# Filler matmuls at the start of TensorE's queue, and two small loads moved to GpSimd's queue, in an RWKV-and-MLP kernel

## The chip, the cores and the metric

The kernel runs on one core of one Trainium2 chip. The metric is the device time of one execution in microseconds (us). Engines are named as the profile names them: PE is TensorE (matmuls), PEld its weight loads, DVE is VectorE, ACT is ScalarE, POOL is GpSimd, SP is SyncE, which here only issues transfers.

## The reference, cut to what matters

```python
# r, k, v: (4, 8, 768, 48); w, u: (8, 48)
for t in range(S):
    cur = einsum('bhd,bhe->bhde', u[None] * k_t, v_t)
    y[:, :, t] = einsum('bhd,bhde->bhe', r_t, state + cur)
    state = w[None, :, :, None] * state + einsum('bhd,bhe->bhde', k_t, v_t)
x = y.transpose(0, 2, 1, 3).reshape(3072, 384)
out = square(maximum(x @ moe_w_in, 0)) @ moe_w_out     # (384, 2048), (2048, 384)
```

A linear recurrence with a decay w and a bonus u, and then a two-layer block with a squared ReLU.

## The kernel before, in words

The sequence of 768 steps is cut into 6 chunks of 128 for each of 4 batches: 24 units, numbered 4 x chunk + batch. Within a chunk the recurrence is written as masked products, and between the chunks of a batch a state is carried.

Each unit goes through these steps. SP loads r, k and v (L288). DVE multiplies r and k by powers of w (`scale`, L311, once for r and once for k); these powers, `wpos` and `wneg`, come once from a chain at the start: a row of w is loaded by ACT's queue (L205), ACT takes its logarithm (L222), PE spreads it over the partitions in one f32 product (`spread_log`, L260), and ACT raises it (L263). The scaled r and k are transposed, by PE (`turn`, L331, eight 128x128 transposes in two groups of four, each evicted by ACT, L335) for the first seven units, and by a DMA transpose (L320) for the rest. DVE multiplies the transposed pair (`rk`, L340). PE makes the 128x128 products of r and k (`at`, L348), DVE masks them (`mask`, L360, twice). PE makes `sums` (L368 with the columns of u, and L373, which gives what is added to the state). DVE forms `dv` (L382) and the state (`state_add`, L390 in the first chunk, L392 later; `state_decay`, L396), ACT casts the state (L402). PE makes y (L411 and L417), DVE evicts it (L426). y is transposed by PE (L442) with an eviction by ACT (L446), or by a DMA transpose (L435). PE then multiplies by `w_in` (`mm1`, L458, steps of 12 matmuls of 128 columns, or 6 of 256 where two units are taken together), ACT applies the ReLU (L466), DVE or ACT squares (L475, L473), PE multiplies by `w_out` (`mm2`, L482, steps of 4 matmuls of 384 columns; L497 for the last unit), ACT evicts (L489), and SP stores (L519).

Once, near the start, w and u are also loaded as columns: `columns` (L255, L256) issues two loads of 4 x 2 x 48 numbers on SP's queue, `spread_columns` (L268) transposes them on PE in f32, DVE copies them (`copy_columns`, L271), and POOL makes of them the matrix `uwb` for `sums` (L274, L277) and the decay over a chunk, `wend` (L280, L282), for `state_add`.

The weights are loaded in quarters on POOL's queue (`weights`), w_in at L298 and w_out at L302, with a cast to bf16. Before each, POOL copies one number of a unit's k tile (`gate`, L294), so that the weights start after that unit's loads.

The order of all work is not left to a scheduler. Every step is entered in a `Plan` with an engine, a cost, what it needs, a rank and its buffers. `Plan.run` goes through time with these costs and, for each engine, starts the ready step of the lowest rank; the instructions are then emitted in that order, which is the order in which each engine runs them. A step marked `move` is a transfer, with an issue cost and a time to land. The eight PSUM banks are handed out by the plan too, with a limit for each kind. In the order that comes out for PE, log is first, then the first four transposes of unit 0, the column transposes, the other four, and so on; on SP the column loads stand between the loads of unit 0 and unit 1.

Of the kernel before, what the change touches and what calls it, by code (L numbers as in the profile page):

```python
# [149 lines left out]
def kernel(  # L150
# [11 lines left out]
    nc = tc.nc  # L162
# [42 lines left out]
    nc.scalar.dma_start(out=wrow, in_=w.rearrange("h d -> (h d)").unsqueeze(0))  # L205
    nc.scalar.preload_act_table_set("natural_log_exp_and_others")
    wu = const.tile([HP, 2, 2, 64], F32)
    nc.vector.memset(wu[:, 0], 1.0)
# [38 lines left out]

    w_in_sb = const.tile([128, NK, dff], BF16)
    w_out_sb = const.tile([128, NF, dm], BF16)
    gate = const.tile([128, 1], F32)  # L250
# [3 lines left out]
    def columns():  # L254
        nc.sync.dma_start(out=wu[:, 0, :, :D], in_=w.rearrange("(p o) d -> p o d", o=2))  # L255
        nc.sync.dma_start(out=wu[:, 1, :, :D], in_=u.rearrange("(p o) d -> p o d", o=2))  # L256

# [35 lines left out]
    def weights(i, q, which):  # L293
        nc.gpsimd.tensor_copy(gate, tiles[i]["kt"][:, 0, :1])  # L294
        if which == "I":
            sl = slice(q * dff // NQ, (q + 1) * dff // NQ)
            src = moe_w_in.rearrange("(ko ki) f -> ki ko f", ki=128)
            nc.gpsimd.dma_start(out=w_in_sb[:, :, sl], in_=src[:, :, sl])  # L298
        else:
            sl = slice(q * NF // NQ, (q + 1) * NF // NQ)  # L300
            src = moe_w_out.rearrange("(ko ki) f -> ki ko f", ki=128)
            nc.gpsimd.dma_start(out=w_out_sb[:, sl, :], in_=src[:, sl, :])  # L302

# [144 lines left out]
    def mm1(i, m, s):  # L448
        c, b = units[i]
        t = tiles[i]  # L450
        if b == 0 and s == 0:
            chunks[c]["g"] = gpool.tile([128, NF, B, C], BF16, name="g")
        t["h", s] = bank("h", i, s).rearrange("p (a u c) -> p a u c", u=m, c=C)
        for a in range(4 // m):
            f = s * (4 // m) + a
            for n in range(NK):
                turned = w_in_sb[:, n, f * 128 : (f + 1) * 128]
                nc.tensor.matmul(  # L458
                    out=t["h", s][:, a], lhsT=turned, rhs=chunks[c]["xT"][:, n, b : b + m, :],
                    start=(n == 0), stop=(n == NK - 1),  # L460
                )
# [15 lines left out]
    def mm2(i, q):  # L477
        t = tiles[i]
        if q == 0:
            t["o"] = bank("o", i)[:, :dm]  # L480
        for f in range(q * 4, q * 4 + 4):
            nc.tensor.matmul(  # L482
                out=t["o"], lhsT=chunks[units[i][0]]["g"][:, f, units[i][1], :], rhs=w_out_sb[:, f, :],
                start=(f == 0), stop=(f == NF - 1),
            )
# [5 lines left out]
    def mm2_half(i, n):  # L491
        t = tiles[i]
        if n == 0:
            t["o"] = bank("o", i)[:, :dm]
        sl = slice(n * dm // 2, (n + 1) * dm // 2)
        for f in range(NF):
            nc.tensor.matmul(  # L497
                out=t["o"][:, sl], lhsT=chunks[units[i][0]]["g"][:, f, units[i][1], :], rhs=w_out_sb[:, f, sl],
                start=(f == 0), stop=(f == NF - 1), skip_group_check=True,
            )  # L500
# [34 lines left out]
    copy("begin", SP, 0.74, None, rank=-1e3)  # L535
    copy("wu", SP, 1.46, columns, rank=-99.75, move=(0.1, 16, 0.67, 0.1))
    add("cols", PE, 0.1, spread_columns, rank=-50, needs=["wu"], new=[("h", "cols")])
# [141 lines left out]
    )  # L679
    for s in plan.run(room, dict(at=4, s=2, y=2, h=4, o=2), len(banks)):  # L680
        if s["emit"] is not None:
# [31 lines left out]
```

## Time and profile before

| what | us |
|---|---|
| three runs | 180.97, 183.15, 185.44 |
| their median | 183.15 |
| the profiled execution | 179.87 |
| its span, first to last instruction | 178.1 |
| PE busy | 163.5 |
| DVE busy | 144.8 |
| ACT busy | 118.8 |
| POOL busy | 12.4 |

The profile is one execution. A line of instructions in order of time gives the start, the busy time, the engine, the source line, the operation, what it writes and reads with shapes, how many instructions were merged, and in brackets how long the engine had stood idle before and what released it. An engine name with a q (SPq, POOLq) is its queue of transfers. DVE, ACT and POOL run their instructions in the order given; a wait at the head of a queue holds up all that stands behind it.

### The profile page before, as it was taken

Reading aid. Unit: us, or ns where it says so; the run is one execution under the profiler, and the core shown is the slowest. Engines: PE = TensorE matmul, PEld = TensorE weight load, DVE = VectorE, ACT = ScalarE, POOL = GpSimd, SP = SyncE. Lnnn points to the kernel's source line nnn. Section 1 sums busy time; section 2 is a strip of 40 time slices with the busy share of each in tenths; the row PEclk is TensorE's granted clock in tenths of the full one; section 3 lists DMA queues with packets and bytes.
Section 4 is the critical chain, followed back from the end, with each engine's and each line's share of the span. In section 5 each row is a group of like instructions: output and inputs, shape, how many; then the busy total and the mean of one; then the engine's idle time right before and its main releaser. Section 6 shows DMA issues by size and latency. Waiting matters only on the chain.

```text
span 178.1 us, 4914 instructions
## 1 busy us (share of the span) xinstructions
PE 163.5 (92%) x1982; PEld 125.2 (70%) x1982; DVE 144.8 (81%) x307; ACT 118.8 (67%) x240; POOL 12.4 (7%) x38
## 2 busy tenths in 40 slices
PE   2477889999999999999999999998999999999992
PEld 1356679886687886686786775784875788777771
DVE  4398998855899999999799999998998799762310
ACT  4546889987464965696694594694691897746620
POOL 3250950000000000000000000000000000000000
PEclk9999999999999999999999999999999999999999
DMA  5899999999955889999998899999999999811212
GB/s 116 161 184 202 171 200 187 184 202 184 129 107 95 155 158 197 118 207 213 137 206 180 167 193 159 207 188 135 222 199 137 216 163 208 235 47 26 90 62 70
DMA packets 107680, 28.56 MB, mean 160 GB/s; under 512 B 100873, under 2 KB 107658, under 8 KB 107658
## 3 DMA queue, kind: packets, MB, share of 16 engines
q1 hardware_dynamic: 103944, 25.11, 79.7%
q0 software_dynamic: 3712, 3.15, 11.0%
q8 instruction: 15, 0.25, 0.6%
q14 instruction: 7, 0.06, 0.1%
q10 hardware_dynamic: 2, 0.00, 0.0%
HBM read 20.45 MB, written 4.72 MB: 141 GB/s over the span
## 4 chain that ended last, share of the span: by engine, by line
PE 59%; DMA 21%; DVE 11%; ACT 3%; issue 2%; SPq 2%; ACTq 0%
PE bank L458 26%; PE bank L482 20%; DMA rkT<-rkw 12%; DMA xT<-yb 4%; PE bank L348 3%; DMA rt<-in_r_dram 3%; DVE rkw L311 3%; DMA kt<-in_k_dram 2%; PE bank L331 2%; DVE am L360 2%; DVE g L475 2%; PE bank L411 2%; DVE yb L426 2%; PE bank L497 1%; ACT rkT L335 1%
## 5 line engine op out<-in xcount | busy, mean ns | idle before, releaser
L458 PE MATMUL bank<-xT,w_in_sb 128*128 128x128 bf16 (+1 forms) x864 | 73.4, 238 | 0.3
L482 PE MATMUL bank<-w_out_sb,g 128*128 128x384 bf16 x368 | 68.3, 326 | 0.0
L466 ACT ACTIVATE gr<-bank 128x512 f32<-128x512 f32 x96 | 55.0, 594 | 18.9 <-PE bank L458 16.3
L458 PEld LDWEIGHTS <-w_in_sb 128*128 128x128 bf16 x864 | 61.2, 98 | 7.5 <-issue 0.5
L475 DVE TENSOR_TENSOR g<-gr 128x512 bf16<-128x512 f32 x64 | 43.1, 685 | 12.9 <-ACT gr L466 12.8
L482 PEld LDWEIGHTS <-g 128*128 128x128 bf16 x368 | 33.3, 98 | 18.1 <-DVE g L475 0.2
L360 DVE TENSOR_TENSOR am<-bank,smask 128x512 bf16<-128x512 f32 x48 | 31.7, 684 | 1.1 <-PE bank L348 0.7
L402 ACT CAST stb<-st 64x192 bf16<-64x192 f32 x40 | 13.9, 348 | 15.5 <-DVE st L396 14.6
L473 ACT ACTIVATE g<-gr 128x512 bf16<-128x512 f32 x32 | 20.1, 632 | 0.8
L489 ACT COPY osb<-bank 128x384 f32<-128x384 f32 x23 | 11.0, 478 | 8.4 <-PE bank L482 8.1
L311 DVE TENSOR_TENSOR rkw<-rt,wpos 128x384 bf16<-128x384 f32 x24 | 13.2, 550 | 3.0 <-ACT wpos L263 2.5
L426 DVE TENSOR_TENSOR yb<-bank,dv 128x384 bf16<-128x384 f32 x24 | 13.3, 553 | 1.3 <-PE bank L417 0.9
L311 DVE TENSOR_TENSOR rkw<-kt,wneg 128x384 bf16<-128x384 f32 x24 | 13.2, 551 | 1.3 <-DMA kt<-in_k_dram 1.3
L382 DVE TENSOR_TENSOR dv<-vb,bank 128x384 f32<-128x384 bf16 x24 | 13.1, 546 | 0.5 <-PE bank L373 0.5
L348 PE MATMUL bank<-rkT 64*128 64x128 bf16 x192 | 10.2, 229 | 3.6 <-ACT rkT L335 2.0
L340 DVE TENSOR_TENSOR rk<-rkT 128x512 bf16<-128x512 bf16 x24 | 10.1, 420 | 3.8 <-ACT rkT L335 1.9
L348 PEld LDWEIGHTS <-rkT 64*128 64x128 bf16 x192 | 5.8, 98 | 9.5 <-DMA rkT<-rkw 3.9
L315 ACT CAST vb<-vt 128x384 bf16<-128x384 f32 x24 | 12.2, 509 | 0.2
L335 ACT COPY rkT<-bank 128x512 bf16<-128x512 bf16 x14 | 8.2, 584 | 5.9 <-PE bank L331 5.6
L392 DVE TENSOR_TENSOR st<-bank,st 64x192 f32<-64x192 f32 x32 | 11.3, 352 | 0.2
L331 PE MATMUL bank<-identb,rkw 128*128 128x128 bf16 x56 | 6.7, 256 | 3.6 <-DVE rkw L311 1.8
L411 PEld LDWEIGHTS <-am 128*128 128x128 bf16 x192 | 8.4, 98 | 1.7 <-DVE am L360 0.3
(52 smaller groups left out, 90.2 us busy)
## 6 DMA issues: line engine op xcount, KB each, us to landing
rt<-in_r_dram SPq DMA_DIRECT2D x24, 192.0 KB, 3.1
kt<-in_k_dram SPq DMA_DIRECT2D x24, 192.0 KB, 3.8
vt<-in_v_dram SPq DMA_DIRECT2D x24, 192.0 KB, 4.0
out_dram<-osb SPq DMA_DIRECT2D x23, 192.0 KB, 2.9
w_in_sb<-in_moe_w_in_dram POOLq DMA_DIRECT2D x4, 384.0 KB, 7.6
w_out_sb<-in_moe_w_out_dram POOLq DMA_DIRECT2D x4, 384.0 KB, 13.8
xT<-yb SPq DMA_TRANSPOSE x18, 3.6
rkT<-rkw SPq DMA_TRANSPOSE x17, 3.7
```

Of the source, the lines that this page charges most:

```text
L311: nc.vector.tensor_tensor(t["rkw"][:, x, :, :, :D], pair(src), pair(wx), ALU.mult)
L315: nc.scalar.copy(tiles[i]["vb"], tiles[i]["vt"])
L348: nc.tensor.matmul(out=t["at"][o][:, p, :], lhsT=t["rkT"][sl, 1, p, :], rhs=t["rkT"][sl, 0, p, :], start=True, stop=True,)
L360: nc.vector.tensor_tensor(am, t["at"][o], smask.unsqueeze(1).to_broadcast([C, HP, C]), ALU.mult)
L382: nc.vector.tensor_tensor(t["dv"], t["vb"], t["d"].unsqueeze(2).to_broadcast([C, H, D]), ALU.mult)
L402: nc.scalar.copy(stb[b][sl, :, o * D : (o + 1) * D], st32[b][sl])
L426: nc.vector.tensor_tensor(t["yb"], t["y"], t["dv"].rearrange("p h d -> p (h d)"), ALU.add)
L458: nc.tensor.matmul(out=t["h", s][:, a], lhsT=turned, rhs=chunks[c]["xT"][:, n, b : b + m, :], start=(n == 0), stop=(n == NK - 1),)
L466: nc.scalar.activation(t["gr", s], t["h", s], AF.Relu)
L473: nc.scalar.activation(g, x, AF.Square)
L475: nc.vector.tensor_tensor(g, x, x, ALU.mult)
L482: nc.tensor.matmul(out=t["o"], lhsT=chunks[units[i][0]]["g"][:, f, units[i][1], :], rhs=w_out_sb[:, f, :], start=(f == 0), stop=(f == NF - 1),
```

## The change

A tile `warm` of ones (128 x 256, bf16) is set by DVE first of all. Sixty fillers, each one matmul of 256 columns of that tile by itself into a bank of its own that nothing reads, are entered in the plan for PE with the highest ranks, each needing the one before it, so that they are placed wherever the plan has nothing else ready for PE; the ninth also needs log. The loads of w and u as columns are issued on POOL's queue with a planned issue cost of 4.4 us instead of SP's with 1.46. The weights become one tile for each quarter, with the same transfers and the same reads.

In the order that comes out, PE runs 8 fillers, log, 5 fillers, the column transposes, 2 fillers, the first four transposes of unit 0, 2 fillers, the other four, 5 fillers, the first four transposes of unit 1, 2 fillers, `at` of unit 0, 1 filler, `sums` of unit 0, 1 filler, the other four transposes of unit 1, 8 fillers, `at` of unit 1, y of unit 0, 10 fillers, the x transposes of unit 0, 3 fillers, and so on; all sixty stand ahead of the first step of `mm1`. On DVE the copy of the columns moves ahead of the k scaling of unit 0, the r scaling of unit 1 ahead of `rk` of unit 0. On PE, y of unit 3 moves behind the second-quarter steps of `mm1` of units 0 and 1. On POOL the two column loads follow the memset of `uwb` and stand ahead of the work on the columns and of all weight gates. On SP the loads of unit 1 follow those of unit 0 directly. Later steps keep their kind of order but change places by a step or two on all engines.

```diff
+    warm = const.tile([128, 256], BF16)
+    nc.vector.memset(warm, 1.0)
     wu = const.tile([HP, 2, 2, 64], F32)
...
-    w_in_sb = const.tile([128, NK, dff], BF16)
-    w_out_sb = const.tile([128, NF, dm], BF16)
+    w_in_q = [const.tile([128, NK, dff // NQ], BF16, name=f"w_in_q{q}") for q in range(NQ)]
+    w_out_q = [const.tile([128, NF // NQ, dm], BF16, name=f"w_out_q{q}") for q in range(NQ)]
...
     def columns():
-        nc.sync.dma_start(out=wu[:, 0, :, :D], in_=w.rearrange("(p o) d -> p o d", o=2))
-        nc.sync.dma_start(out=wu[:, 1, :, :D], in_=u.rearrange("(p o) d -> p o d", o=2))
+        nc.gpsimd.dma_start(out=wu[:, 0, :, :D], in_=w.rearrange("(p o) d -> p o d", o=2))
+        nc.gpsimd.dma_start(out=wu[:, 1, :, :D], in_=u.rearrange("(p o) d -> p o d", o=2))
+
+    def fill():
+        nc.tensor.matmul(out=bank("fill")[:, :256], lhsT=warm[:, :128], rhs=warm, start=True, stop=True)
...
-            nc.gpsimd.dma_start(out=w_in_sb[:, :, sl], in_=src[:, :, sl])
+            nc.gpsimd.dma_start(out=w_in_q[q], in_=src[:, :, q * dff // NQ : (q + 1) * dff // NQ])
...
-    copy("wu", SP, 1.46, columns, rank=-99.75, move=(0.1, 16, 0.67, 0.1))
+    copy("wu", POOL, 4.4, columns, rank=-99.75, move=(0.1, 16, 0.67, 0.1))
+    add("made", PE, 1.25, None, rank=-2e3)
+    for n in range(60):
+        add(
+            ("fill", n), PE, 0.215 if n < 16 else 0.108, fill, rank=1e3 + n, needs=[("fill", n - 1) if n else "made", "log" if n == 8 else None],
+            new=() if n else [("fill",)], uses=[("fill",)] if n else (),
+        )
...
-    for s in plan.run(room, dict(at=4, s=2, y=2, h=4, o=2), len(banks)):
+    for s in plan.run(room, dict(at=4, s=2, y=2, h=4, o=2, fill=1), len(banks)):
```

## The prediction, made before the changed kernel was run

> **What bounds the kernel now.** I read the page's slices first, then a table of busy time by stage, then the instructions in order of time through the first 25 us, where all edits lie.
>
> From the page, the span in 40 slices of 4.45 us:
>
> ```profile
> PE   2477889999999999999999999998999999999992
> DVE  4398998855899999999799999998998799762310
> PEclk9999999999999999999999999999999999999999
> ```
>
> The table by stage (stretch, its length, then busy us and instructions of PE, PEld, DVE, ACT, POOL, then clock and DMA):
>
> ```profile
> core 0: us, PE busy (x) PEld busy (x) DVE busy (x) ACT busy (x) POOL busy (x), PEclk, DMA share, GB/s
> 5.40:9.38 3.98, 2.29 (x25) 1.65 (x26) 2.01 (x6) 2.05 (x4) 1.72 (x7) 1.00 1.05 184
> 9.38:15.30 5.92, 4.04 (x47) 3.08 (x45) 5.85 (x13) 3.29 (x8) 1.95 (x6) 1.00 1.27 182
> 15.30:25.00 9.70, 7.84 (x120) 6.40 (x118) 9.12 (x20) 7.90 (x17) 7.24 (x14) 1.00 1.20 193
> 25.00:60.00 35.00, 34.98 (x519) 28.71 (x517) 29.04 (x59) 26.62 (x55) 0.00 (x0) 1.00 0.99 161
> 60.00:160.00 100.00, 98.08 (x1134) 73.60 (x1132) 92.88 (x190) 69.29 (x143) 0.00 (x0) 1.00 0.98 176
> ```
>
> From 25.0 us on TensorE is the bound: 34.98 of 35 us busy, then 98.08 of 100. What the front can give is therefore the moment at which TensorE becomes saturated, about 25 us, and nothing of TensorE's busy time before it counts by itself. From 9.38 to 25 us VectorE is the bound (5.85 of 5.92, 9.12 of 9.70). Before 9.38 it is one chain through all engines.
>
> The instructions in order of time, first 12 us (start, duration, engine, line, idle before and its releaser):
>
> ```profile
> 3.91 0.63 SPq L256 DMA_DIRECT2D wu<-in_u_dram  x1
> 4.59 0.44 SPq L288 DMA_DIRECT2D rt<-in_r_dram  x1
> ...
> 6.04 0.61 PE L331 MATMUL bank<-identb,rkw 128*128 128x128 bf16 x4 [1.27 <-DVE rkw L311]
> ...
> 6.58 0.37 PE L268 MATMUL bank<-ident,wu 4*128 4x4 f32 x2
> ...
> 8.56 0.43 DVE L340 TENSOR_TENSOR rk<-rkT 128x512 bf16<-128x512 bf16 x1 [1.41 <-ACT rkT L335]
> ...
> 10.65 0.92 POOL L298 DMA_DIRECT2D w_in_sb<-in_moe_w_in_dram  x1
> ```
>
> and from 12 to 24 us:
>
> ```profile
> 15.75 0.55 DVE L382 TENSOR_TENSOR dv<-vb,bank 128x384 f32<-128x384 bf16 x1 [0.46 <-PE bank L373]
> ...
> 16.95 1.46 PE L458 MATMUL bank<-xT,w_in_sb 128*128 128x128 bf16 x12
> ...
> 19.00 0.40 PE L331 MATMUL bank<-identb,rkw 128*128 128x128 bf16 x4
> ...
> 19.46 0.83 PE L458 MATMUL bank<-xT,w_in_sb 128*128 128x128 bf16 x12
> ```
>
> and TensorE alone after 24 us:
>
> ```profile
> 24.84 0.27 PE L411 MATMUL bank<-vb,am 128*128 128x48 bf16 x4 [0.24 <-DVE am L360]
> 24.96 2.17 PE L458 MATMUL bank<-xT,w_in_sb 128*128 128x128 bf16 x36
> ```
>
> Here one sees TensorE change speed at about 19 us although the clock row shows 9 throughout: four transposes take 0.61 us before and 0.40 after, twelve L458 matmuls 1.46 and 0.83. The state followed a stretch in which PE was busy 3.20 of 3.41 us (15.69 to 19.10); the two stretches of that length before it, busy 2.38 and 2.51, did not bring it. VectorE stood 1.41 us before rk (L340) and 0.46 us before dv (L382), both behind slow TensorE groups. TensorE's saturated stretch starts at 24.96, right after y of unit 3 had waited 0.24 us for a mask.
>
> **The change part by part.** Times are those of the profiled execution: 179.87 us, span 178.1 and 1.77 around it. It lies under all three runs (180.97, 183.15, 185.44).
>
> 1. *Columns on GpSimd's queue.* GpSimd is free at 2.30 (the uwb memset, 2.17 + 0.13). Its weight loads cost 0.74 to 0.92 us to issue; two of them end at about 4.0. After the issue at 10.65 that queue moved no data until 13.2, that is 2.55 us after the issue began. So the second, issued at about 3.2, moves data at 5.8 and is seen at about 6.2. Lower end: nothing shows a load of 8 rows on this queue; if its issue cost little and it landed as SP's do (3.0 us from issue, median), 5.3. Upper end: as the fastest whole weight load (6.3 us after its issue), 9.5. I take 6.2, since the 1.5 KB behave like the first data of a load, not like all of one. Behind that wait: on TensorE the two column transposes now stand ahead of the first real work (eight fillers, log, five fillers, columns, two fillers, then the first transposes of unit 0); on VectorE the copy of the columns stands ahead of the k scaling of unit 0. Columns 6.2 + 0.37, gap 0.06, two fillers at 0.11 to 0.21 each: the transposes of unit 0 begin at about 6.9 instead of 6.04, **0.9 us late**. On GpSimd itself nothing is delayed: it waited 4.94 us for the copied columns before (7.24), and what is queued behind (uwb, wend, the first weight gate) follows the copy, now at about 6.7 instead of 6.99; the first weight load goes out at about 10.3 instead of 10.65.
> 2. *On SP* the two issues go (1.18 + 0.63, from 2.68 to 4.59). Unit 1's r is issued at about 2.7, and later loads move up by some 0.8 us, since the DMA engines were busy except about 4.8 to 5.8. That covers the loads which the first weight gates read (the second gate waited 5.75 us for k of unit 3, to 17.31). w_in's second quarter comes about 0.7 us earlier. Worth nothing alone: hidden by VectorE's stage, but it keeps the weights from being late when the rest moves up.
> 3. *TensorE faster early.* Eight fillers from about 1.1 to 2.9, log 3.13 to 4.77, five fillers to 5.8: TensorE is nearly always busy, so the full speed should come before 9 us rather than at 19. A transpose group then costs 0.40 instead of 0.61, the eight L348 matmuls 0.40 (21.65) instead of 0.61. Two transpose groups stand in the chain before rk: 2 x 0.21 = 0.4 back of the 0.9. rk starts at about 8.56 + 0.5 = 9.05.
> 4. *VectorE's new order.* The r scaling of unit 1 (pitch 0.47) moves ahead of rk, into the idle 1.41 us. So dv of unit 0 starts 2.0 us after rk, not 2.48: 11.05, against 11.04 before. Parts 1, 3 and 4 cancel: **0.0** (ends: -0.8 if the columns land at 5.3, +3.3 if at 9.5).
> 5. *VectorE's gaps.* From 9.38 to 25 it stood 0.07 + 0.58 = 0.65 us, of which 0.46 before dv of unit 1 behind slow groups. At full speed most of it closes: **-0.5** (ends: 0 and -0.65).
> 6. *Order before saturation.* y of unit 3 and its 0.24 us wait move behind two w_in steps; the steps of units 0 and 1 on the second quarter start after the transposes of unit 4. The 0.24 wait and part of the 0.27 behind it come off: **-0.4** (ends 0 and -0.5). The remaining TensorE work is the same.
> 7. *Sixty fillers.* All stand before the first w_in step. Between 9.38 and 15.3 TensorE was idle 5.92 - 4.04 = 1.88 us. At full speed the 4.04 shrinks by about a third, to some 2.7, leaving 3.2; the 30 or so fillers there cost 30 x 0.107 = 3.2 (a slow step of 12 x 128 columns took 1.46, with some 0.2 for the last one to come out: 0.105 for 128 columns, 0.21 for a filler's 256, half of it at full speed). They just fit: **+0.1** (ends 0 and +1.7, one stretch of 3.4 us at half speed).
> 8. *Tiles for each quarter of the weights*: the same transfers and reads of the same shapes. The first w_in step ran at 16.95 before the second quarter was issued (17.77), so no wait hangs on the single tile: 0.
> 9. *The memset of warm* (0.17, as L208) lies in VectorE's idle 2.55 us before 5.42: 0.
>
> Sum: 0.0 - 0.5 - 0.4 + 0.1 = -0.8; w_in's earlier quarter allows it. The planner lists later steps in a changed order too: work ahead of each unit's steps on TensorE shifts by up to one w_in step, 0.65 us, either way. 179.87 becomes about 179.1. The four executions shown average (179.87 + 180.97 + 183.15 + 185.44)/4 = 182.36; less 0.8 and a little for runs in which TensorE sped up later than in this profile, I forecast 181.4 for the median of runs.
>
> [...]
>
> [...]
>
> **The rivals.**
>
> *A. The columns land late (slower).* Place: head of TensorE's queue. Every microsecond past 6.2 delays unit 0, and with it the saturated VectorE stage. At 7.0 the gain is gone; at 9.5, 179.1 + 3.3 = 182.4 in the profile, some 184.7 in the runs; over 2% slower (186.8) needs about 11.6. For: the transfer has been seen to take 6.3 us with much data. Against: 1.5 KB.
>
> *B. The fillers run at half speed.* If TensorE does not reach full speed by about 9 us, 30 fillers cost 6.4 us against 1.88 us of idle time. One slow stretch of 3.4 us costs 1.7: 180.8 in the profile, 183.1 in the runs. Against: such a stretch would be all busy and end the state.
>
> *C. The speed-up tames the runs.* The profile is lower than all runs. If slower runs are those in which full speed came later than 19 us, fillers bring all runs to the best front: 178 to 179.4. For: 5.6 us between executions, and a start that hangs on how densely small groups follow. Against: the front explains 2 or 3 us at most.
>
> *D. The later order takes it back.* From 60 to 160 us TensorE stands 1.92 us, and transposes by DMA hold 12.4% of the chain. A step issued 0.65 us early before its transpose has landed waits; a handful of these costs 1 to 4 us: 183 to 186 in the runs.
>
> **How the numbers follow.** Forecast 0.43 (own range 179.0 to 183.4), A 0.12, B 0.08, C 0.24, D 0.13. The range 177.6 to 186.0 leaves out the far ends of C, A and D. A change under 2% is about what a measurement of this kernel cannot tell from none, that is 179.5 to 186.8. Faster: C and the low end of the forecast, 0.30. Slower: the far part of A and D, and runs that spread upward, 0.17. Within: 0.53.
>
> **What would show it.** Right: groups L331 at 0.40 us before 9 us; column transposes at 6.2 to 6.6; rk at 9.0; VectorE without the 0.46 gap; the saturated stretch starting at about 24.1. Wrong: TensorE idle over 0.8 us ahead of the columns (A); L331 groups at 0.6 after 9 us with fillers on both sides (B); runs within 1% of each other (C); more than 2 us of TensorE idle time from 60 to 160 us (D).

## The result, and the profile after

| | before | after |
|---|---|---|
| median of 20 runs each | 181.70 us | 183.72 us |
| lowest to highest | 180.11 to 185.44 | 182.00 to 187.51 |
| profiled execution, its span | 179.87, 178.1 | 184.31, 182.5 |

The ratio after to before is 1.0109, 95% interval 1.0082 to 1.0136: about 2 us slower, where 0.8 us of gain had been forecast. The ratios here and below leave out executions with a disturbed clock or an outlying time, so they can differ from the quotient of the medians.

The table of busy time by stage, of the changed kernel (stretch, its length, then busy us and instructions of PE, PEld, DVE, ACT, POOL, then clock and DMA):

```profile
5.40:9.38 3.98, 2.95 (x18) 1.94 (x17) 1.67 (x4) 1.04 (x2) 1.51 (x6) 1.00 1.13 199
9.38:15.30 5.92, 5.92 (x68) 4.45 (x67) 4.11 (x9) 3.28 (x7) 2.58 (x9) 1.00 1.17 169
15.30:25.00 9.70, 7.46 (x118) 6.01 (x117) 9.24 (x21) 7.48 (x16) 6.35 (x13) 1.00 1.21 202
25.00:60.00 35.00, 34.84 (x529) 28.90 (x526) 29.70 (x61) 27.25 (x57) 0.00 (x0) 1.00 0.89 152
60.00:160.00 100.00, 95.35 (x1101) 71.56 (x1098) 90.67 (x187) 65.53 (x140) 0.00 (x0) 1.00 0.92 175
```

From 9.38 to 15.30, where VectorE had been busy 5.85 us, it is busy 4.11 and TensorE 5.92, all of the stretch. 27 of TensorE's 68 matmuls there are fillers, busy 4.52 us: the chain waits for TensorE, which is at fillers. From 60 to 160 us TensorE is busy 95.35 us, not 98.08.

The instructions in order of time, first POOL's and the column steps, then TensorE around the first two units, then the start of VectorE's chain:

```profile
2.24 0.75 POOL L257 DMA_DIRECT2D wu<-in_w_dram  x1
2.98 0.61 POOL L258 DMA_DIRECT2D wu<-in_u_dram  x1
7.53 0.44 POOL L279 TENSOR_TENSOR cols<-cols 128x4 f32<-128x4 f32 x1 [3.93 <-DVE cols L276]
11.12 0.80 POOL L302 DMA_DIRECT2D w_in_q<-in_moe_w_in_dram  x1
14.65 0.18 POOL L299 COPY gate<-kt 128x1 f32<-128x1 f32 x1 [2.73 <-DMA kt<-in_k_dram]
```

```profile
6.73 0.50 PE L273 MATMUL bank<-ident,wu 4*128 4x4 f32 x2 [0.78 <-DMA wu<-in_w_dram]
7.16 0.61 PE L261 MATMUL bank<-warm 128*128 128x256 bf16 x2
7.56 0.63 PE L334 MATMUL bank<-identb,rkw 128*128 128x128 bf16 x4
7.99 0.63 PE L261 MATMUL bank<-warm 128*128 128x256 bf16 x2
8.87 0.59 PE L334 MATMUL bank<-identb,rkw 128*128 128x128 bf16 x4 [0.25 <-ACT rkT L338]
9.24 1.27 PE L261 MATMUL bank<-warm 128*128 128x256 bf16 x5
10.31 0.63 PE L334 MATMUL bank<-identb,rkw 128*128 128x128 bf16 x4
10.74 0.63 PE L261 MATMUL bank<-warm 128*128 128x256 bf16 x2
11.30 0.61 PE L351 MATMUL bank<-rkT 64*128 64x128 bf16 x8
...
12.52 0.39 PE L334 MATMUL bank<-identb,rkw 128*128 128x128 bf16 x4
```

```profile
10.11 0.43 DVE L343 TENSOR_TENSOR rk<-rkT 128x512 bf16<-128x512 bf16 x1 [1.73 <-ACT rkT L338]
13.22 0.54 DVE L385 TENSOR_TENSOR dv<-vb,bank 128x384 f32<-128x384 bf16 x1
```

The busy time of a group of matmuls runs past the start of the next group (the two fillers at 7.16 are busy 0.61 us, and the transposes start 0.40 behind them), so what a group costs is read from one start to the next. TensorE stands 0.78 us ahead of the columns. Then transposes and fillers alternate at half speed (0.63 us for four transposes), full speed (0.39) coming at 12.3 us only. `at` of unit 0 (L351) starts at 11.30. `rk` of unit 0 starts at 10.11 (8.56 before) and `dv` at 13.22 (11.04 before), 2.2 us late. The second weight gate opens at 14.65, 2.66 us earlier than before. On TensorE the saturated stretch starts at 26.22, against 24.96:

```profile
24.84 0.83 PE L461 MATMUL bank<-xT,w_in_q 128*128 128x128 bf16 x12 [0.66 <-ACT xT L449]
...
26.22 1.50 PE L461 MATMUL bank<-xT,w_in_q 128*128 128x128 bf16 x24
```

This is the fourth step of 12 matmuls on w_in in both kernels. So 1.26 us of the loss are there at 26 us. From 24.84 on neither kernel's TensorE has a wait of over 0.1 us before 30 us; but by 24.84 it had started 181 matmuls before the change and 150, without the fillers, after it. The same lag, 1.2 us, is found at the y evictions of units 6 to 9. The rest of this execution's 4.4 us comes after 70 us, where TensorE's waits for transposes by DMA are 2.6 us (1.6 before), with 1.8 us of others. Of the 20 executions 7 had a mean granted clock under 0.993, of the 35 of the kernel before in a later batch 2; 5 of the 20 took 2.5 us or more above the fastest. (Two expectations below have 8 for these counts.)

### The profile page after: what moved, and what is told of

It reads as the page before. It is cut to its first block, busy times and chain, and to the rows that moved or that the text cites. A ratio compares the mean times of both kernels' runs of the same rounds, so it can differ in the third digit from the quotient of the medians.

```text
span 182.5 us, 5020 instructions
## 1 busy us (share of the span) xinstructions
PE 169.7 (93%) x2042; PEld 129.5 (71%) x2042; DVE 144.7 (79%) x308; ACT 116.3 (64%) x240; POOL 13.2 (7%) x40
## 3 DMA queue, kind: packets, MB, share of 16 engines
q0 software_dynamic: 3776, 3.15, 10.9%
## 4 chain that ended last, share of the span: by engine, by line
PE 66%; DMA 15%; DVE 11%; ACT 4%; issue 2%; POOL 1%; POOLq 0%
PE bank L485 27%; PE bank L461 23%; DMA rkT<-rkw 10%; PE bank L351 3%; DVE g L478 3%; DVE am L363 3%; DMA xT<-yb 3%; PE bank L261 2%; DMA wu<-in_w_dram 2%; PE bank L414 2%; PE bank L334 2%; PE bank L376 2%; DVE rkw L314 2%; DVE yb L429 1%; PE bank L500 1%
## 5 line engine op out<-in xcount | busy, mean ns | idle before, releaser
L461 PE MATMUL bank<-xT,w_in_q 128*128 128x128 bf16 (+1 forms) x864 | 71.3, 237 | 1.0 <-ACT xT L449 0.9
L485 PE MATMUL bank<-w_out_q,g 128*128 128x384 bf16 x368 | 68.7, 326 | 0.0
L469 ACT ACTIVATE gr<-bank 128x512 f32<-128x512 f32 x96 | 54.1, 599 | 20.3 <-PE bank L461 19.1
L461 PEld LDWEIGHTS <-w_in_q 128*128 128x128 bf16 x864 | 61.1, 98 | 7.5 <-issue 1.1
L343 DVE TENSOR_TENSOR rk<-rkT 128x512 bf16<-128x512 bf16 x24 | 10.1, 421 | 5.7 <-DMA rkT<-rkw 3.9
L351 PE MATMUL bank<-rkT 64*128 64x128 bf16 x192 | 9.7, 222 | 4.3 <-DMA rkT<-rkw 2.6
L261 PE MATMUL bank<-warm 128*128 128x256 bf16 x60 | 11.8, 332 | 1.2 <-DVE warm L208 1.2
L351 PEld LDWEIGHTS <-rkT 64*128 64x128 bf16 x192 | 5.5, 95 | 9.9 <-DMA rkT<-rkw 5.0
L318 ACT CAST vb<-vt 128x384 bf16<-128x384 f32 x24 | 12.3, 512 | 0.1
## 6 DMA issues: line engine op xcount, KB each, us to landing
w_out_q<-in_moe_w_out_dram POOLq DMA_DIRECT2D x4, 384.0 KB, 14.3
```

What stands on the lines that cost most here:

```text
L261: nc.tensor.matmul(out=bank("fill")[:, :256], lhsT=warm[:, :128], rhs=warm, start=True, stop=True)
L351: nc.tensor.matmul(out=t["at"][o][:, p, :], lhsT=t["rkT"][sl, 1, p, :], rhs=t["rkT"][sl, 0, p, :], start=True, stop=True,)
L461: nc.tensor.matmul(out=t["h", s][:, a], lhsT=turned, rhs=chunks[c]["xT"][:, n, b : b + m, :], start=(n == 0), stop=(n == NK - 1),)
L469: nc.scalar.activation(t["gr", s], t["h", s], AF.Relu)
L485: nc.tensor.matmul(out=t["o"], lhsT=chunks[units[i][0]]["g"][:, f, units[i][1], :], rhs=w_out_q[f // 4][:, f % 4, :], start=(f == 0), stop ...
```

## The experiments

Five theories stand in the expectations; their letters are not those of the prediction's rivals. *C*: the columns on GpSimd's queue land late and hold up TensorE, and the work on the columns holds up the first weight load. *F*: fillers at half speed stand in the way of the first units. *K*: what counts is when TensorE's clock steps up and whether it falls back (its 0.92, in an expectation below, is the window from 15.45 to 18.86 us of the kernel before, busy 3.15 of 3.41 us; its fall back is seen in the kernel without fillers, where four transposes took 0.39 us at 21.66 and 0.63 at 25.30, behind idle times of 0.74 and 0.85 us; where the steps lie is told in the last section). *G* (formed on the way): SP's earlier loads open the weight gate earlier, and the weight streams then hold back k of unit 4. *L*: the later order costs (the prediction's rival D), or, in the last run, late waits that vary between executions. "Low clock" below is a mean granted clock under 0.993 in an execution. One stretch of 3.41 us at half speed in a span of 178 makes 0.990.

### The parts one at a time

*The changed kernel, fillers entered in the plan but not issued:*

```diff
-            ("fill", n), PE, 0.215 if n < 16 else 0.108, fill, ...
+            ("fill", n), PE, 0.215 if n < 16 else 0.108, None, ...
```

> The changed kernel with its own order on every engine, but the sixty fillers are not issued (the plan still reserves their time). Theory C, the wait for the columns at the head of TensorE's and VectorE's queues is what costs: the front stays late, rk of unit 0 at 9.5 us or later, and the kernel stays 1.5 to 2.5 us slower than before. Theory F, the fillers in front of real work cost (they hold 2.5% of the chain of waits of the changed kernel, 4.5 us): rk of unit 0 at 9 us, the 1.3 us before the transposes of unit 1 gone, and the kernel gets back at least 1.3 of its 2 us. Theory L, the later order costs: still 2 us slower, with over 3 us of TensorE idle time from 60 to 160 us.

Measured: 182.25 against 181.31 us, ratio 1.0062 (1.0024 to 1.0099). So the rest of the change is slower without the fillers too, and the 60 fillers add some 0.5% in this order (the intervals of 1.0062 and 1.0109 overlap). VectorE's chain in its profile:

```profile
10.09 0.42 DVE L343 TENSOR_TENSOR rk<-rkT 128x512 bf16<-128x512 bf16 x1 [1.31 <-ACT rkT L338]
12.10 0.54 DVE L385 TENSOR_TENSOR dv<-vb,bank 128x384 f32<-128x384 bf16 x1
```

`rk` of unit 0 is as late as with the fillers, as theory C has it (here the load of u landed at 7.33, 0.4 us later than in the changed kernel). But `dv` follows 2.01 us behind `rk`, and 3.11 with the fillers: 1.1 us of `dv`'s lag is theirs, which is theory F's part.

*The kernel before with only the column loads moved, its order kept:*

```diff
-        nc.sync.dma_start(out=wu[:, 0, :, :D], ...)
+        nc.gpsimd.dma_start(out=wu[:, 0, :, :D], ...)
```

> The kernel before with its order, only the two column loads are issued on GpSimd's queue. The columns were seen by TensorE at 6.73 us in the changed kernel; in the order of before they stand behind the first transposes of unit 0, which end at 6.65. Theory C: no more than 0.3 us slower, since nothing waits at the head; the loads of unit 1 come 0.8 us earlier and VectorE's r scaling of unit 1 cannot use it, so 0 to 0.5 us faster is as likely. Theories F and L: the same, within 0.5 us of before.

Measured: 184.54 against 181.31, ratio 1.0077 (1.0028 to 1.0127). Alone this edit costs 0.8%, where all three theories had 0.5 us or less. Its TensorE in order of time:

```profile
16.59 0.50 PE L411 MATMUL bank<-vb,am 128*128 128x48 bf16 x8
18.19 1.03 PE L458 MATMUL bank<-xT,w_in_sb 128*128 128x128 bf16 x8 [1.10 <-DMA w_in_sb<-in_moe_w_in_dram]
```

The first `mm1` step waits 1.10 us for w_in and starts at 18.19, not 16.95. The first weight load goes out at 11.07, 0.42 us later, since on GpSimd the six squarings of `wend` follow the later columns and stand ahead of the gate; and it lands 7.1 us after its issue, not 6.3, while the second gate opens at 14.41 instead of 17.31. Full speed comes at 22.1 us, not 18.9, and the saturated stretch starts at 26.32, though `dv` of unit 0 is only 0.16 us late. This is another way to lose than the changed kernel's: there w_in landed at 17.4, and the first `mm1` step, at 19.23, did not wait for it.

*The two orders joined at the first `mm1` step on w_in's second quarter* (columns on GpSimd's queue in both): first the front of before with the later order of after, then the front of after with the later order of before.

```diff
+    order = front + [s for s in rest if s["key"] not in seen]
```

> The order of before up to the first w_in step of the second quarter (no fillers, columns on GpSimd's queue), the order of the changed kernel from there on. Theories C and F (the front costs): as fast as the kernel before, within 0.6 us. Theory L (the later order costs): slower than before by 1.5 to 3 us, ratio 1.008 to 1.016, with more TensorE idle time from 60 to 160 us than the 1.92 us of before.

> The order of the changed kernel with its fillers up to the first w_in step of the second quarter, the order of before from there on. Theories C and F: slower than before by 1.2 to 2.1 us, ratio 1.007 to 1.012, since yb of units 0 to 2 came 2.1 us late and of units 6 to 9 1.2 us late. Theory L: within 0.6 us of before.

Measured: 1.0034 (0.9993 to 1.0075) and 1.0037 (1.0 to 1.0074). Against the kernel with the same front, the later order of after takes 0.4% off once (1.0077 to 1.0034) and adds 0.7% once (1.0037 to 1.0109). Both are some 0.6 us slower than before: for the first that is what theories C and F had, for the second what theory L had. The later order has no effect of one sign, and neither half carries the loss alone.

### Fillers without the columns' move

*The kernel before, 13 fillers early (8 ahead of log, 5 ahead of the first transposes), order otherwise kept:*

```diff
+    FILLERS = {"log": 8, ("turn", 0, 0): 5}
```

> The kernel before, its columns on SP and its order, with 13 fillers only: eight ahead of log and five behind it, where TensorE stood idle from 1.2 to 3.1 and from 4.8 to 6.0 us. Nothing waits for them. Theory K (the clock: full speed follows a window of 3.41 us in which TensorE is 0.92 busy or more, windows run freely, and half speed comes back after one that is 0.54 busy or less): the five behind log end at 6.0, the windows after that are 0.45 to 0.75 busy as before, so full speed still comes near 19 us, and the time is that of before, within 0.5 us. If any work on TensorE counts for good, full speed by 9 us and 0.5 to 1 us faster.

Measured: 1.0077 (1.0047 to 1.0107). In the profile its front is that of the kernel before to 0.1 us through unit 9, and full speed comes at 20.7 us (eight `at` matmuls still take 0.61 us at 15.89). The loss lies after 70 us. Theory K has the front right; that the kernel is 0.8% slower, with the same front and the same order, none of the theories has, and it is not explained.

*The same with 24 fillers, put only where the profile before shows TensorE idle:*

```diff
+    FILLERS = {
+        "log": 8, ("turn", 0, 0): 5, ("turn", 0, 1): 1, ("at", 0): 3, ("turn", 1, 1): 2, ("at", 1): 1,
+        ("xturn", 0): 1, ("turn", 2, 1): 2, ("at", 2): 1,
+    }
```

> The kernel before, its columns on SP and its order, with 24 fillers at the places at which TensorE stood idle up to 15.9 us, sized by those gaps at half speed. Theory K: windows up to 12 us come to 0.9 and more, full speed comes by 9 to 13 us, VectorE's 0.46 us gap goes, no column is late, and the kernel is 0.3 to 1.2 us faster than before, less what a return to half speed near 25 us costs (1.7 us in the runs that have it). Theory F, fillers in front of real work cost whatever the clock does: 0.5 us slower or more.

> The kernel with 24 fillers and the columns on SP's queue once more, on another chip. Its front is, to 0.1 us, that of the kernel with the columns issued early on GpSimd's queue (1.002), yet it measured 0.991. If its first measurement stands (theory: even harmless-looking columns on GpSimd's queue cost 1% somewhere late): 0.988 to 0.995 again. If six runs happened to fall on executions with few late waits for the transposed k and r of the DMA queue (theory L: these waits vary by 3 us between executions whatever the kernel): 0.995 to 1.002, with runs spread from 178.5 to 183.

Measured: 179.08 us, 0.991 (0.9876 to 0.9945), and on another chip 179.27 us, 0.9888 (0.9832 to 0.9945). This is faster than both kernels. Full speed comes at 10.5 us, the front is 0.5 us earlier, and the gain in the runs, 2.1 and 2.6 us, is larger than that:

```profile
10.85 0.38 PE L337 MATMUL bank<-identb,rkw 128*128 128x128 bf16 x4 [0.25 <-ACT rkT L341]
...
24.36 0.27 PE L417 MATMUL bank<-vb,am 128*128 128x48 bf16 x4 [0.33 <-DVE am L366]
24.47 2.17 PE L464 MATMUL bank<-xT,w_in_sb 128*128 128x128 bf16 x36
```

*The changed kernel with the column loads kept on SP's queue* (planned there too, so that the order differs a little):

```diff
-    copy("wu", POOL, 4.4, columns, rank=-99.75, move=(0.1, 16, 0.67, 0.1))
+    copy("wu", SP, 1.46, columns, rank=-99.75, move=(0.1, 16, 0.67, 0.1))
```

> The changed kernel with sixty fillers, but the column loads stay on SP's queue with the planned cost that they had; the plan then places them behind the first transposes of unit 0 and makes an order of its own. Theory C (the columns' late landing, at 6.9 us for the second, delays unit 0 and, by way of uwb and wend, the first weight load to 11.1): rk of unit 0 at 8.6 to 8.9 us instead of 10.1, and 1 to 2 us of the loss gone, ratio to before 0.998 to 1.005. Theories F and K (fillers or clock): still 1.5 us slower than before or more.

Measured: 1.0023 (0.9992 to 1.0054), medians 182.80 against 181.22. `rk` starts at 8.73 us, as theory C had it, and full speed comes at 9.8; but `dv` starts at 11.90, 3.17 us behind `rk`, and 11 of 12 executions had low clock. In the profile TensorE falls to half speed from 23.43 to 26.85 us. The table of busy time for that stretch and the one before it:

```profile
20.02:23.43 3.41, 1.64 (x30) 1.08 (x27) 3.35 (x9) 3.26 (x8) 3.41 (x7) 1.00 1.21 200
23.43:26.85 3.42, 3.06 (x36) 2.93 (x36) 2.91 (x7) 2.08 (x5) 0.22 (x1) 0.50 1.21 191
```

At full speed TensorE has little to do while VectorE is the bound: busy 1.64 of 3.41 us, then a clock of 0.50. The fillers end at 16.5 us and do not help there.

*The changed kernel with 13 fillers more in the gaps from 20 to 24 us:*

```diff
+    FILLERS = {("turn", 3, 1): 2, ("at", 3): 4, ("xturn", 2): 2, ("m1", 2, 0): 5}
```

> The changed kernel with 13 more fillers in TensorE's idle stretches between 22 and 24.8 us (ahead of the second transposes of unit 3, at and the x transposes of unit 2, the first w_in step of unit 2). Theory K: no window there is as empty as 0.54, half speed no longer returns near 25 us, no run has a mean clock under 0.992 (8 of 20 runs of the changed kernel had), and the median falls by 0.5 to 1 us, ratio to before 1.005 to 1.008. If the clock is not part of it: as the changed kernel, ratio 1.009 to 1.013, or slower by the fillers' 1.5 us.

Measured: 1.0118 (1.0063 to 1.0174): nothing gained. In its profile VectorE waits 3.40 us for k of unit 4 before a scale step, and TensorE with it:

```profile
27.13 0.56 DVE L314 TENSOR_TENSOR rkw<-kt,wneg 128x384 bf16<-128x384 f32 x1 [3.40 <-DMA kt<-in_k_dram]
```

TensorE falls to half speed from 27.22 to 34.04 (mean clock 0.90 from 25 to 60 us). Thirteen fillers can't cover a load that is late. Theory G comes from this row.

### The column move on top of fillers that work

*The kernel with 24 fillers, columns on GpSimd's queue (the diff of the columns alone):*

> The faster kernel with 24 fillers at TensorE's gaps in the old order (0.991), with the loads of w and u as columns issued from GpSimd's queue and nothing else altered: what the column move alone costs where TensorE's clock is at full speed from 10.5 us anyway. Theory C (columns land at 6.6 to 7.2 us and GpSimd's column work, then the first weight load, follow): first weight load at about 11.1 instead of 10.5, first m1 step of unit 0 waits on w_in for about 1 us, saturated stretch from 25.2 to 25.6 instead of 24.5, ratio 0.996 to 1.000. Theory G adds: unit 3's k lands at about 14.5, second weight load issued at about 15, unit 4's k at 23 to 24 us, one run in three 1.7 us longer, ratio 1.000 to 1.008. If the column move costs nothing: 0.989 to 0.993.

Measured: 0.9972 (0.9927 to 1.0017), 181.78 us; 7 of 12 executions with low clock, three of them at 186 to 187 us. The move costs 0.6 to 0.8% again. The profile caught one of the three (186.07 us). VectorE, then TensorE, in order of time:

```profile
22.42 0.55 DVE L317 TENSOR_TENSOR rkw<-rt,wpos 128x384 bf16<-128x384 f32 x1
26.35 0.56 DVE L317 TENSOR_TENSOR rkw<-kt,wneg 128x384 bf16<-128x384 f32 x1 [3.39 <-DMA kt<-in_k_dram]
```

```profile
23.25 0.83 PE L464 MATMUL bank<-xT,w_in_sb 128*128 128x128 bf16 x12
27.30 0.27 PE L374 MATMUL bank<-uwb,rk 128*128 128x8 bf16 x4 [3.21 <-DVE rk L346]
```

and the same kernel's table by stage for windows of 3.41 us (PEclk is the last column but two):

```profile
19.18:22.59 3.41, 2.36 (x39) 1.79 (x39) 3.35 (x8) 3.34 (x8) 2.59 (x5) 1.00 1.20 202
22.59:26.00 3.41, 1.07 (x16) 0.90 (x16) 0.38 (x1) 1.66 (x4) 0.00 (x0) 1.00 1.22 187
26.00:29.42 3.42, 2.11 (x28) 1.99 (x29) 3.04 (x7) 0.81 (x2) 0.00 (x0) 0.50 1.27 184
29.42:32.83 3.41, 3.41 (x34) 3.31 (x32) 2.92 (x6) 1.67 (x4) 0.00 (x0) 0.50 1.27 184
```

k of unit 4 lands near 26 us. The second gate of this kernel opened at 14.57; with the columns on SP's queue it opened at 16.36 in one profile and at 15.18 in the other. TensorE is busy 1.07 of 3.41 us, and the next two windows run at half speed. Theory G's chain is seen whole in this execution and in that of the kernel with 13 fillers more: early gate, late k, idle TensorE, lower clock. The profiles of all kernels with the columns on GpSimd's queue bear out its first link: k of unit 4 landed between 19.4 and 27.1 us in the seven whose second gate opened at 14.3 to 14.7, and between 19.7 and 20.6 in the seven whose gate opened at 15.9 or later.

*The later weight gates moved to other loads.* First to k of unit 4, in the changed kernel, in the last kernel and in the one with 24 fillers and columns on SP's queue:

```diff
-        nc.gpsimd.tensor_copy(gate, tiles[i]["kt"][:, 0, :1])
+        nc.gpsimd.tensor_copy(gate, tiles[i if i < 3 else 4]["kt"][:, 0, :1])
```

> The changed kernel, with one tile name altered: the gates of weight quarters 2 to 4 of w_in and of all of w_out read k of unit 4 instead of k of unit 3, so these streams can't start before unit 4's k has landed. Theory G (the earlier loads open the weight gate at 14.7 instead of 17.3 us, and the weight streams then hold back unit 4's k from 20.0 to about 23.9 us): k of unit 4 lands at 19 to 20.5 us, the second weight load is issued at 19 to 21 instead of 15.1, the wait of a scale step of unit 4 on it (0.5 us in the profile of the changed kernel) goes, fewer than one run in five is 2.5 us or more above the fastest (8 of 20 before), and the ratio to the kernel before falls from 1.011 to about 1.004 to 1.007. Theory C+F (late columns and slow fillers ahead of the first log product, 2.0 us of front): the ratio stays at 1.009 to 1.013. Rival: the second quarter of w_in is itself late now and the first step that needs it waits: a wait of 1 us or more on a w_in tile at 25 to 30 us, and a ratio of 1.012 or more.

> As the kernel with 24 fillers and the columns on GpSimd's queue, and the gates of the later weight quarters read k of unit 4. Theory G: back to the front's part of the loss alone, ratio 0.994 to 0.999, with k of unit 4 at 19 to 20.5 us and no window of half clock after 12 us. Theory C alone: no different from the kernel without the gate's change, within 0.3%.

> The faster kernel with 24 fillers, columns on SP's queue, and the gates of the later weight quarters on k of unit 4. There k of unit 3 lands at 16.4 us and unit 4's k at 20 or soon after, so theory G expects little: the second weight load at 19.5 to 21 instead of 16.8, unit 4's k 0 to 1 us earlier, ratio 0.988 to 0.993, with a spread over the runs of under 2 us. Rival: the weights come late instead, a wait of 1 us or more on a w_in tile at 24 to 30 us, and a ratio of 0.995 or more.

Measured: 1.0197 (1.0149 to 1.0246), 1.0142 (1.0081 to 1.0202), 1.0053 (1.0012 to 1.0095). All are slower than the same kernels with the old gate, as the rival in the expectations has it: the gate opened at 19.8 to 21.4 us, and now w_in's second quarter is late. In the profile of the kernel with the columns on SP's queue:

```profile
28.49 4.02 PE L464 MATMUL bank<-xT,w_in_sb 128*128 128x128 bf16 x36 [3.17 <-DMA w_in_sb<-in_moe_w_in_dram]
```

Then to r of unit 4, which was expected to open them at 16.5 to 18:

```diff
-        nc.gpsimd.tensor_copy(gate, tiles[i]["kt"][:, 0, :1])
+        nc.gpsimd.tensor_copy(gate, tiles[i]["kt"][:, 0, :1] if i < 3 else tiles[4]["rt"][:, 0, :1])
```

> The kernel with 24 fillers and the columns issued at 2.25 us on GpSimd's queue (0.997, and 4 of 12 runs at 183 to 187 us), with the gates on r of unit 4. Theory G: second weight load at 16.5 to 18, unit 4's k at 19 to 21, the long runs go (at most one in ten 4 us above the fastest), ratio of the undisturbed runs 0.994 to 0.998, which is theory C's part. Theory C alone: long runs stay.

> The changed kernel with the gates of the later weight quarters on r of unit 4. Theory G: second weight load at 16.5 to 18 instead of 15.1, unit 4's k at 19.5 to 21.5 instead of 23.9, ratio 1.004 to 1.008 instead of 1.011. If unit 4's k is no part of the changed kernel's loss: 1.009 to 1.013. Rival, as in the run with the gate on k of unit 4: the w_in quarters come late, a wait of 0.8 us or more on w_in, 1.015 or more.

Measured: 1.0003 (0.9947 to 1.0058) and 1.0114 (1.0072 to 1.0156). r landed later than expected, and the gates opened at 18.5 and 19.7 us. With the 24 fillers the executions with low clock fell from 7 of 12 to 1 of 12, and none was over 184 us, as theory G says. (These were two chips; on one chip, with the columns issued early, below, they fell from 5 of 12 to 1 of 12.) But the saturated stretch begins with a wait of 1.39 us for w_in at 25.96, so the median stays (181.72). In the changed kernel nothing is won, and 3 of its 6 executions still had low clock, in the profile with k of unit 4 landed in time, at 20.4 us. So with 24 fillers the early gate makes the long executions; for the changed kernel this is not shown, and the other executions win nothing by a later gate.

### The columns early on GpSimd's queue

*The two loads issued ahead of GpSimd's masks* (issue from 1.61 us instead of 2.24), in the kernel with 24 fillers, in the same with the gates on r of unit 4, and in the changed kernel:

```diff
+    nc.gpsimd.dma_start(out=wu[:, 0, :, :D], in_=w.rearrange("(p o) d -> p o d", o=2))
+    nc.gpsimd.dma_start(out=wu[:, 1, :, :D], in_=u.rearrange("(p o) d -> p o d", o=2))
     iota_i = const.tile([128, 1], mybir.dt.int32)
```

> The kernel with 24 fillers and the columns on GpSimd's queue (0.997), but the two loads are issued as GpSimd's third and fourth instructions, at about 1.2 us, before its masks, instead of at 2.25 and 3.0. So the columns are no longer late while SP's queue is still freed. Theory C (the loss of the column move is the columns' lateness): columns' transposes at 5.5 to 6.2, first weight load at 10.0 to 10.5, ratio back to 0.988 to 0.993. Theory G (the loss is that SP's earlier loads open the weight gate early and unit 4's k comes late): second weight load still at 14.5 to 15.2, unit 4's k at 22 us or later, one run in four 4 us or more longer, ratio of the undisturbed runs 0.990 to 0.997.

> As the kernel with the columns early on GpSimd's queue, and the gates of weight quarters 2 to 4 and of w_out read r of unit 4 (issued at about 12 us), which should open them at 16.5 to 18, as in the kernel before (17.3), not at 14.6 as now nor at 20 to 21 as with unit 4's k. Theories C and G together: neither loss is left, ratio 0.985 to 0.992, no run 4 us above the fastest. Theory C alone: as without the gate's change.

> The changed kernel with the two column loads issued at about 1.2 us on GpSimd's queue, ahead of its masks; its order and its 60 fillers stay. Theory C (the columns' lateness is most of the changed kernel's loss): columns' transposes at 5.5 to 6.2 instead of 6.73, first log-dependent step rk(0) at 9.3 to 9.7 instead of 10.1, saturated stretch at 25.2 to 25.8 instead of 26.2, ratio 1.002 to 1.007. Theory F (fillers at half speed ahead of the chain) keeps rk(0) at 10.0 or later and the ratio at 1.009 to 1.013.

Measured, in this order: 1.0017 (0.9972 to 1.0062), 0.998 (0.9939 to 1.0021), 0.9994 (0.9929 to 1.006). In the changed kernel the columns are transposed at 5.88 without a wait, `rk` starts at 9.22 instead of 10.11 and the saturated stretch at 25.72 instead of 26.22; `dv` starts at 12.34, still 3.12 us behind `rk`. The ratio rests on 4 of the 12 executions; the medians of all are 182.72 against 181.90 (1.0045), so about half of the loss or more is back, as theory C expects.

In the kernel with 24 fillers theory C, which had 0.988 to 0.993, fails. Its front is the one with the columns on SP's queue to 0.05 us (saturated stretch at 24.43 and 24.44), the gate opens at 15.92, and still its ratio is 1.1 to 1.3% higher. With the gate on r of unit 4 as well, C and G together had 0.985 to 0.992; it came to 0.998, with a wait of 1.10 us for w_in at 25.96 in its profile. TensorE's waits from 70 us on, first with the columns early on GpSimd's queue, then on SP's:

```profile
PE bank L355 <- DMA rkT<-rkw: 4.5, 6, 1.0
```

```profile
PE bank L354 <- DMA rkT<-rkw: 1.8, 3, 0.6
```

These are waits for the scaled r and k of units 7 and later, transposed by DMA from SP's queue. From the y eviction of unit 9 to TensorE's last instruction the two executions take 106.9 and 104.7 us. Over the 20 profiles this tail lies between 104.0 and 107.6, in both orders.

## Why the prediction was wrong, point by point

*Step 4, "Parts 1, 3 and 4 cancel: 0.0", failed.* `dv` of unit 0 came at 13.22, not 11.05: the term is +2.2, inside its ends (-0.8, +3.3). Three pieces make it up: unit 0's transposes began 0.66 us later than forecast (7.56, not 6.9), the 0.40 us of faster transposes did not come, and `dv` followed 3.11 us behind `rk`, not 2.0.

- *Step 1, the landing, was mis-sized.* The second load was issued at 2.98 and landed 3.9 us later, not 3.0. The columns were transposed from 6.73, not 6.2; the next start came 0.43 us behind, as forecast (0.37 + 0.06), and the two fillers took 0.40 (7.16 to 7.56), the slow end of my 0.11 to 0.21 each. GpSimd, "nothing is delayed", was 0.5 us late with the first weight load (11.12; before 10.65, and I had 10.3), since the copy of the columns came at 7.27. That cost nothing in this kernel.
- *Step 3, "the full speed should come before 9 us", failed.* It came at 12.3, so the 0.40 us never came back.
- *Step 4 left out what stands ahead of `at`.* Its "2.0 us after rk" counts VectorE's order alone. The transposed pair of unit 0 was there at about 10.1 (the eviction at 9.49 took 0.59 us), but `at` started at 11.30 only, behind five fillers, unit 1's transposes and two fillers. Before, it had started as the eviction ended. The eviction after the change, then the eviction and `at` before it:

```profile
9.49 0.59 ACT L338 COPY rkT<-bank 128x512 bf16<-128x512 bf16 x1 [0.67 <-PE bank L334]
```

```profile
7.95 0.59 ACT L335 COPY rkT<-bank 128x512 bf16<-128x512 bf16 x1 [0.67 <-PE bank L331]
8.59 0.61 PE L348 MATMUL bank<-rkT 64*128 64x128 bf16 x8 [0.68 <-ACT rkT L335]
```

The changed kernel without fillers shows this piece by itself: `dv` 2.01 us behind `rk`, the 2.0 of the forecast. The two fillers between unit 0's groups cost nothing: behind them TensorE stood 0.25 us more, for ACT. This piece and step 3 are rival B, which I gave 0.08 because a busy stretch "would end the state"; its sign, groups at 0.6 after 9 us with fillers on both sides, was there.

*Step 2, SP's queue.* Right that the loads move up (unit 1's r from 4.59 to 2.67). I had w_in's second quarter 0.7 us earlier for it; the gate opened 2.66 us earlier. "Worth nothing alone" overlooked that k of unit 4 can land late then. What that costs is shown in long executions of two kernels, the one with 24 fillers and the changed one with 13 more. In the profile of the changed kernel itself k of unit 4 landed at 23.9 and was used at 24.76, without a wait.

*Steps 5 and 6.* I forecast -0.5 and -0.4. From `dv` of unit 0 to the saturated stretch the lag shrank from 2.2 to 1.26, so 0.9 us did come back. The sum fits, by luck. `dv` of units 1 to 3 was still 2.0 to 2.1 us late, and VectorE's gaps did not close as step 5 has it (idle 0.46 of 9.70 us after 15.3, against 0.58): step 5 gave 0.1 of its 0.5. The other 0.8 came behind it, where TensorE's order is another (step 6, and y of unit 3 is not yet done at 26.22); step 6 was not tried alone. My premise, that only the moment of saturation counts, also left out that work not done by then has to be done after it: the waits end at 24.84 in both kernels, but with 181 matmuls started and with 150.

*Step 7, fillers +0.1.* Without them the changed kernel is 0.5% faster, some 0.9 us. "They just fit" held for full speed only: behind 12.3 us the lag of `dv` grew no more. Steps 8 and 9 were not tried alone; no wait in the profile hangs on them.

*The rivals.* A holds in part: TensorE stood 0.78 us ahead of the columns, its sign being over 0.8, and the column move costs 0.6 to 0.9% in each of three pairs (alone 1.0077; with 24 fillers 0.991 and 0.989 to 0.997; the changed order 1.0023 to 1.0109), though in the old order by a wait for w_in and in the changed one at the head of the queue. Rival C fails: the runs spread over 5.5 us. D's sign, over 2 us of idle TensorE from 60 to 160, was there (4.65 us), but the kernel with 13 fillers in the old order has as much (4.70 us, 4.2 of it waits for DMA transposes), so the sign can't tell D from chance.

*What stays open.* Shown is the front: 1.26 us at 26 us, of which 0.5 came back with the columns issued early, and 1.1 us of `dv`'s lag that went with the fillers. The rest of the loss, after 70 us, is not explained. The kernel with 13 fillers, 0.8% slower with the front and the order of before, warns that a ratio of that size need not come from the front. Why the kernel with 24 fillers loses 1% after 70 us when its columns are issued from GpSimd, with the same front, is not known; nor why it is faster by more than its front when they are on SP's queue. The late waits for DMA transposes are where it shows.

The range of 177.6 to 186.0 held the 183.72, in part by luck. The forecast took 1.0 us off an average of 182.36, and the change put 2.0 on: a miss of 3.0 us, 2.1 of it in the front (-0.8 forecast, +1.26 measured). The centre was only 2.3 us too low, because the average stood 0.7 above the median of 20 runs, 181.70.

## What to carry to other kernels

Fillers pay only where the engine would stand idle at the speed it has at that moment, and not ahead of the first useful work: 24 of them in measured gaps took 1% off, 60 wherever the plan saw room put some on. Count, for each one, which real step stands behind it in the queue, and when that step's inputs are there. Before a small load moves to another queue, follow both queues: what stands behind the load on the new one, and which gate the freed queue opens earlier. A term that "cancels" out of three uncertain parts deserves the width of all three.

## What the runs showed of the hardware that was not expected

*The clock.* Where TensorE's speed fell, it did so for 3.41 us or twice that: with 60 fillers and the columns on SP's queue it was at half speed from 23.43 to 26.85, with 24 fillers and the columns on GpSimd's queue from 26.00 to 32.83. The phase of the steps differs between executions: the one at 12.3 in the changed kernel and the one at 23.43 lie 11.1 us apart, 3.25 times 3.41. The windows ahead of the two falls were busy 1.64 and 1.07 of 3.41 us (above); no fall came behind 2.14 (changed kernel, 22.57 to 25.98), nor behind 2.57 and 2.65 (kernel before, 18.86 to 25.68). Full speed came behind windows busy 3.15 us (kernel before, 15.45 to 18.86) and 3.41 (changed kernel, 8.93 to 12.34), not behind 2.44 and 2.50 (kernel before, 8.63 to 15.45), and of the times given above 9.8 us is the earliest. But early busy windows did not bring it: in the changed kernel the one from 2.11 to 5.52 was busy 3.36 us with fillers and the f32 product of one row, and four transposes still took 0.63 us at 7.56. So in the changed kernel with the columns early, where full speed comes at 12.2:

```profile
5.40:8.82 3.42, 3.17 (x20) 2.14 (x19) 1.76 (x4) 1.26 (x3) 1.84 (x6) 1.00 1.31 190
8.82:12.23 3.41, 3.41 (x33) 2.50 (x32) 1.99 (x4) 1.36 (x3) 1.91 (x6) 1.00 1.43 186
```

Both windows ran at half speed by their groups (0.63 us for four transposes), though PEclk, the last column but two, reads 1.00 there: before the first change of clock that column is no evidence.

*Small loads.* A load of 1.5 KB from GpSimd's queue took 0.61 to 0.75 us to issue and landed 3.5 to 4.4 us after its issue began (28 loads in 14 profiles). The first 192 KB loads of r on SP's queue, 128 times as large, landed after 3.0 (median of three, kernel before). The two column issues of the changed kernel took 0.75 and 0.61 us, no longer than the weight loads' 0.74 to 0.92.
